# One attention-and-MLP kernel: the opening pair's scores from unsplit float32 keys and queries, with the bias rows as a four-row product

## The chip, the cores and the metric

The kernel runs on one core of one Trainium2 chip. The metric is the time of one execution in device microseconds (us); lower is better. TensorE (PE) multiplies and transposes, VectorE (DVE), ScalarE (ACT) and GpSimd (POOL) work elementwise, SyncE (SP) issues most transfers.

## What is computed

Attention over 4 batches, 8 heads, 576 positions and 64 channels, with a causal mask and a bias from running sums of `s`; then two MLPs of 2304 tokens, 512 channels and 2048 hidden units. Only the attention's scores matter here:

```python
scores = scale * np.matmul(q, k.transpose(0, 1, 3, 2))
s_pos = np.maximum(s, 0.0)
cum = np.cumsum(s_pos, axis=-1)
bias = -(cum[:, :, :, None] - cum[:, :, None, :])
scores = np.where(causal, -1000000000.0, scores + np.minimum(bias, 0.0))
attn = np.exp(scores - np.max(scores, axis=-1, keepdims=True))
```

## The kernel before

The program has three stages on one PE queue: attention (with the first MLP's first part filled in between from the second batch on), the rest of the first MLP, and the second MLP. Attention works on 16 pairs of heads (`g = 4 * b + p`). Each pair has five units, in the order t = 0, 1, 4, 2, 3; a unit is a block of 128 query rows of both heads (t = 4: the last 64 of both heads in one tile), its score tile as wide as the causal mask lets it be: 128, 256, 576 (as two tiles of 288), 384 and 512 columns.

The order on PE is the order in which the code is written (`attention`, a loop over units j). At step j the score tiles of unit j are made (`unit_scores`, L294), three steps later its exponentials are transposed (`unit_transpose`, L341), one step later multiplied with the values (`unit_values`, L391, float32 on both sides). Between them, in the first steps, stand idle products on zeros (`warm`, L80; `idle` in the profile), 128 x 512 each. On the other engines a scheduler orders the instructions within what the code's `behind(...)` fixes.

Scores are made from split numbers. `prep` (L199) transposes a pair's keys and queries on PE (`tk`, `tq`), ACT rounds them to float32r (`hi`, L213: `kh`, `qs`), DVE makes the remainder (`lo`, L216: into the tile `k2` and the lower half of `qs`). So each tile is 96 channel-by-position blocks of 64 x 288: two halves by head, two by position parity. `kh` is doubled into its lower 64 partitions and `qs` into `k2`; for the first two pairs by POOL (`move`, L251), later by a transfer. The tile `k2` carries, below its 64 channel rows, four bias rows: the running sums, split in two, and the constants 1 and -1. `scores_piece` (L279) then makes two float32r products per score tile: `k2` against `k2` (68 rows: cross terms and bias), behind it `kh` against `qs` (128 rows).

```python
for m, (q, k) in enumerate(((k2[:, 1, h], k2[:, 0, h]), (pr["qs"][:, h], pr["kh"][:, h]))):
```

A score tile narrower than 256 columns is made 256 wide (`max(n, 256)`, L315). DVE then adds the mask and takes the row minimum in one instruction (L319), ACT makes the exponential (L326), DVE the reciprocal of the sums (L336), POOL scales (L339).

The opening: `sums` (L104) makes the running sums in two parts, 256 and 320 positions; each part is split by ACT and DVE (`sum_parts`, L125, staged in `stgA`), and four transfers of it per part go from SP into the first pair's bias rows (`open_rows`, L138). The second part's split stands behind the first head's `lo` instructions (`with self.behind(first)`). Behind the opening pair's last POOL copy, POOL itself issues the third pair's loads (`pair_load`, L168, called at L462). All eight PSUM banks have one tag and are taken in turn.

Of the kernel before, what the change touches and what calls it, by code (L numbers as in the profile page):

```python
# [10 lines left out]
F32 = mybir.dt.float32  # L11
F32R = mybir.dt.float32r
# [3 lines left out]
AF = mybir.ActivationFunctionType  # L16
ALU = mybir.AluOpType
# [8 lines left out]
NB, NH, S, D = 4, 8, 576, 64  # L26
NP = NH // 2
NT = NB * S
DM, DF = 512, 2048
P = 128  # L30
# [18 lines left out]
PARTS = ((0, 256), (256, 576))  # L49
ZEROS = 5  # L50
WARM = 6
RUN_ENDS = ((0, 1, 4, 2, 3), (3,), (3,), (3,))
W2_SLOTS = 7
# [8 lines left out]
class Fused:  # L62
# [136 lines left out]
    def prep(self, att, b, p, ld, first=False):  # L199
        nc, ident = self.nc, self.ident  # L200
        h0, h1 = slice(0, D), slice(D, P)

        def new(nm):
            return att.tile([P, 2, S], F32R, name=f"{nm}{b}_{p}", tag=nm, bufs=2)

        g = b * NP + p
        kh, qs, k2 = new("kh"), new("qs"), self.k2[g % 2]
        self.pairs[b, p] = {"kh": kh, "qs": qs, "k2": k2, "ld": ld, "O": None}  # L210

# [18 lines left out]
        def split(*parts):  # L230
# [10 lines left out]
            for i, (high, low, T, scale) in enumerate(jobs):  # L241
                with self.behind((self.parts[1],) if i else ()):
                    lo(low, T, high, scale)

        def main(nm):
            split(*[turn(nm, h) for h in range(2)])

        def move(o, i, hs=(0, 1)):
            if g < 2:
                for h in hs:  # L250
                    self.copied = nc.gpsimd.tensor_copy(o[:, h], i[:, h].bitcast(F32))  # L251
            else:
                nc.sync.dma_start(o.bitcast(F32), i.bitcast(F32))

        if first:
            turned = [[turn(nm, h) for nm in "kq"] for h in range(2)]
            for h in range(2):
                with self.behind(first):
                    split(*turned[h])
                first = tuple(self.parts)  # L260
                if h == 0:
                    with self.behind(first):
                        first = self.sum_parts(PARTS[1])
                move(kh[h1], kh[h0], (h,))
                move(k2[h0, 1], qs[h0], (h,))
            self.warm(WARM)
            return
        if g > 1:
            self.sum_rows(g, self.rows[g])
        main("k")  # L270
        move(kh[h1], kh[h0])
        yield
        main("q")
        move(k2[h0, 1], qs[h0])
        yield
# [3 lines left out]
    def scores_piece(self, u, sc, hs, j0, w):  # L279
        nc = self.nc  # L280
        b, p, t = u
        pr = self.pairs[b, p]
        for h in hs:
            c0, c1 = t * P, (t + 1) * P
            if t == 4:
                c0, c1 = (S - P if h else S - 64), S
            k2 = pr["k2"][: D + 4]
            for m, (q, k) in enumerate(((k2[:, 1, h], k2[:, 0, h]), (pr["qs"][:, h], pr["kh"][:, h]))):
                nc.tensor.matmul(  # L289
                    sc[: c1 - c0, :w], lhsT=q[:, c0:c1], rhs=k[:, j0 : j0 + w],  # L290
                    start=m == 0, stop=m == 1,
                )

    def unit_scores(self, att, u, h):  # L294
        nc = self.nc
# [17 lines left out]
        else:  # L313
            sc = self.bank("S", f"s{b}_{p}_{t}_{h}")
            self.scores_piece(u, sc, (h,), 0, max(n, 256))  # L315
            j0, w = 0, n
# [21 lines left out]
        for i, bt in enumerate(bts):  # L338
            nc.gpsimd.tensor_scalar(bt[:, :n], bt[:, :n], inv[:, i : i + 1], 1.0, ALU.mult, ALU.mult)  # L339

# [92 lines left out]
    def attention(self, att, mlp):  # L433
# [26 lines left out]
        opened = self.moved  # L460
        with self.behind((self.copied,)):
            loads[2] = self.pair_load(att, 0, 2, eng=nc.gpsimd)  # L462
        later.extend(loads[i]["values"] for i in (1, 2))
        for j in range(n + AHEAD + 1):
# [28 lines left out]
            for _ in tr:  # L493
                pass
            if j < n and idx == 4:
                for _ in nprep:
# [513 lines left out]
```

## Time and profile before

| what | value |
| --- | --- |
| median of 3 runs (lowest, highest) | 1022.94 us (1021.01, 1023.03) |
| the profiled execution's own time, its span | 1021.61 us, 1019.6 us |
| PE busy | 998.2 us (98% of the span) |
| DVE, ACT, POOL busy | 797.3, 718.2, 337.8 us |
| chain that ended last, by engine | PE 89%, DVE 4%, DMA 3%, ACT 2%, issue 1% |
| same chain, the scores' products (L289) | 5% |

The span runs from the first to the last instruction; about 2 us of the execution's own time lie outside it. Starts in the trace count from the span's start. Matmuls are pipelined, so a matmul's row is longer than the step to the next one: what a product costs in a row of products is read from the starts. A float32 product stands as two records in the trace, a float32r product and a transpose as one.

### The profile page before, as it was taken

What the parts mean: (1) busy time and instruction counts of PE and PEld (TensorE: products, weight loads), DVE (VectorE), ACT (ScalarE), POOL (GpSimd) and SP (SyncE); (2) the same over time, 40 slices, a digit from 0 to 9 for tenths busy, and PEclk for the clock granted to TensorE, in tenths of its full rate; (3) what the DMA queues carried; (4) which work ended last, traced back from release to release, by engine and by line L of the source; (5) the groups of instructions that cost most, each with busy time, mean ns of one, the idle gap of its engine ahead of it and who ended that gap; (6) DMA issues with size and microseconds to landing.
All of it is one profiled execution on the core that took longest, in us unless ns stands there. A gap on an engine that the chain in (4) does not pass through costs nothing.

```text
span 1019.6 us, 19822 instructions
## 1 busy us (share of the span) xinstructions
PE 998.2 (98%) x7053; PEld 933.9 (92%) x7054; DVE 797.3 (78%) x1804; ACT 718.2 (70%) x1661; POOL 337.8 (33%) x503
## 2 busy tenths in 40 slices
PE   7889999999999999999999999999999999999997
PEld 4679999999999999999999999999999999989996
DVE  7897666766537977777778747998988989889886
ACT  5999889878756655555555436787887777777775
POOL 5778656554410012222111112232222222222222
PEclk9999999999999999999999999999999999999999
DMA  7664564543237546776666644010010100100000
GB/s 180 157 175 100 135 188 146 152 123 72 59 125 247 177 140 196 230 235 224 212 189 235 208 133 190 1 31 32 3 60 1 32 32 1 63 1 1 32 1 32
DMA packets 79074, 115.97 MB, mean 114 GB/s; under 512 B 25552, under 2 KB 63072, under 8 KB 77440
## 3 DMA queue, kind: packets, MB, share of 16 engines
q1 hardware_dynamic: 72640, 94.94, 31.4%
q0 software_dynamic: 6112, 19.47, 5.1%
q8 instruction: 56, 0.92, 0.4%
q14 instruction: 42, 0.34, 0.1%
q10 hardware_dynamic: 224, 0.30, 0.1%
HBM read 74.78 MB, written 31.60 MB: 104 GB/s over the span
## 4 chain that ended last, share of the span: by engine, by line
PE 89%; DVE 4%; DMA 3%; ACT 2%; issue 1%; POOL 0%; SPq 0%; ACTq 0%; DVEq 0%
PE h L638 38%; PE a L815 19%; PE a L662 19%; PE s L289 5%; PE O L406 4%; PE tp L381 3%; DMA raw<-in_moe_w_in_dram 1%; DVE bt L319 1%; DMA x2p<-st 1%; DVE k L216 1%; PE tq L225 1%; PE tk L225 1%; ACT bt L326 0%; PE tp L360 0%; DVE qs L216 0%
## 5 line engine op out<-in xcount | busy, mean ns | idle before, releaser
L638 PE MATMUL h<-x,u 128*128 128x288 f32 x1536 | 231.5, 296 | 1.2 <-ACT st L677 1.2
L662 PE MATMUL a<-gh,u 128*128 128x288 f32 x1024 | 231.7, 297 | 0.0
L638 PEld LDWEIGHTS h<-x,u 128*128 128x128 f32 x1536 | 212.8, 188 | 3.1 <-ACT st L677 1.5
L798 POOL TENSOR_TENSOR gl<-u,gh 128x384 fp32r<-128x384 f32 x96 | 105.7, 1101 | 290.4 <-ACT gh L796 266.4
L662 PEld LDWEIGHTS a<-gh,u 128*128 128x128 f32 x1024 | 173.0, 188 | 1.1 <-issue 0.5
L638 PE MATMUL h<-y,u 128*128 128x384 f32 x864 | 165.7, 336 | 0.0
L638 PEld LDWEIGHTS h<-y,u 128*128 128x128 f32 x864 | 152.9, 188 | 6.2
L662 PE MATMUL a<-gl,u 128*128 128x288 f32 x512 | 150.0, 295 | 0.7 <-DVE gl L655 0.7
L815 PE MATMUL a<-u,gh 128*128 128x512 f32 x432 | 114.6, 394 | 0.9 <-ACT gh L796 0.9
L649 ACT ACTIVATE g<-h 128x288 f32<-128x288 f32 x128 | 52.0, 407 | 75.8 <-PE h L638 75.4
L724 POOL DMA_DIRECT2D x<-xp x64 | 35.3, 552 | 207.3 <-DVE g L650 106.7
L662 PEld LDWEIGHTS a<-gl,u 128*128 128x128 f32 x512 | 96.5, 188 | 1.4 <-DVE gl L655 0.9
L326 ACT ACTIVATE bt<-bt,mn 128x128 f32<-128x128 f32 (+2 forms) x144 | 84.1, 585 | 19.3 <-DVE mn L319 18.2
L815 PEld LDWEIGHTS a<-u,gh 128*128 128x128 f32 x432 | 80.0, 188 | 14.9 <-ACT gh L796 1.8
L339 POOL TENSOR_SCALAR bt<-bt,sm 128x128 f32<-128x128 f32 (+2 forms) x144 | 81.7, 579 | 30.0 <-DVE sm L336 21.6
L796 ACT ACTIVATE gh<-u 128x384 fp32r<-128x384 f32 x96 | 50.6, 527 | 57.6 <-DVE u L794 56.6
L319 DVE CUSTOM_DVE_ANT_0 bt<-s,mask 128x128 f32<-128x128 f32 (+2 forms) x144 | 68.9, 482 | 27.6 <-PE s L289 25.5
L652 ACT ACTIVATE gh<-g 128x288 fp32r<-128x288 f32 x128 | 56.5, 442 | 45.6 <-DVE g L650 43.8
L650 DVE SCALAR_TENSOR_TENSOR g<-g,h 128x288 f32<-128x288 f32 x128 | 57.5, 450 | 29.8 <-ACT g L649 29.2
L781 ACT ACTIVATE y<-h,cf 128x384 f32<-128x384 f32 x96 | 55.4, 577 | 33.9 <-PE h L638 33.9
L786 DVE SCALAR_TENSOR_TENSOR y<-s,cf,y 128x384 f32<-128x384 f32 x96 | 59.3, 618 | 20.6 <-ACT s L783 19.3
L794 DVE SCALAR_TENSOR_TENSOR u<-y,u 128x384 f32<-128x384 f32 x96 | 73.5, 765 | 1.1
(116 smaller groups left out, 2048.0 us busy)
## 6 DMA issues: line engine op xcount, KB each, us to landing
raw<-in_moe_w_in_dram SPq DMA_DIRECT2D x24, 512.0 KB
raw<-in_moe_w_out_dram SPq DMA_DIRECT2D x24, 512.0 KB
x<-xp POOLq DMA_DIRECT2D x64, 144.0 KB, 3.0
wd<-park POOLq DMA_DIRECT2D x36, 256.0 KB, 4.3
u<-wd SPq DMA_DIRECT2D x8, 1024.0 KB
x2p<-st SPq DMA_DIRECT2D x32, 144.0 KB
xp<-x2p SPq DMA_DIRECT2D x32, 144.0 KB
xp<-x SPq DMA_DIRECT2D x32, 144.0 KB
```

Source lines behind the costliest of these rows:

```text
L319: nc.vector.tensor_tensor_reduce(bt[:, j0 : j0 + w], sc[:, :w], mask, 1.0, 3.0e38 if i == 0 else mn[:, 0:1], ALU.add, ALU.min, mn[:, i : i ...
L326: ex = nc.scalar.activation(bt[:, :n], bt[:, :n], AF.Exp, bias=mn[:, i : i + 1], scale=-1.0, accum_out=sm[:, col : col + 1],)
L339: nc.gpsimd.tensor_scalar(bt[:, :n], bt[:, :n], inv[:, i : i + 1], 1.0, ALU.mult, ALU.mult)
L638: nc.tensor.matmul(ps_tile, lhsT=u[:, wl, kk * P : (kk + 1) * P], rhs=x(xl, kk), start=(n == 0), stop=(n == 3 * KD - 1),)
L650: nc.vector.scalar_tensor_tensor(g[:, :w], g[:, :w], 1.0, h, ALU.add, ALU.mult)
L652: self.newest["act"] = nc.scalar.activation(gh[:, :w], g[:, :w], AF.Copy)
L662: nc.tensor.matmul(acc, lhsT=u[:, wl, d * P : (d + 1) * P], rhs=g[gl], start=(first and i == 0), stop=(last and i == 2),)
L781: nc.scalar.activation(y, h, AF.Abs, scale=cf[:, 4:5])
L786: nc.vector.scalar_tensor_tensor(y, s, cf[:, 7:8], y, ALU.mult, ALU.add)
L794: last = nc.vector.scalar_tensor_tensor(p, y, 2.0, p, ALU.subtract, ALU.mult)
L798: nc.gpsimd.tensor_tensor(gl, p, gh.bitcast(F32), ALU.subtract)
L815: nc.tensor.matmul(accs[m], lhsT=g[gl][:, m * P : (m + 1) * P], rhs=u[:, wl, :], start=(f == 0 and i == 0), stop=(f == NF - 1 and i == 2),)
```

## The change

For the opening pair alone (`PLAIN = 1`) the keys and queries are copied from PSUM to float32 tiles (`keep`, lines 248 to 260 of the changed file) and not split; nothing is doubled into lower partitions. Each score tile of that pair is one float32 product over 64 rows, behind it a float32r product over the four bias rows alone, and it is as wide as the mask lets it be (128 columns for t = 0). The second part of the running sums is split behind the second head's key copies. The third pair's loads are issued by POOL behind the first unit's scaling, at step j = 0.

```diff
@@ -49,6 +49,7 @@
 PARTS = ((0, 256), (256, 576))
 ZEROS = 5
 WARM = 6
+PLAIN = 1
 RUN_ENDS = ((0, 1, 4, 2, 3), (3,), (3,), (3,))
 W2_SLOTS = 7
 LEAD = 2
@@ -200,14 +201,16 @@
         nc, ident = self.nc, self.ident
         h0, h1 = slice(0, D), slice(D, P)
 
-        def new(nm):
-            return att.tile([P, 2, S], F32R, name=f"{nm}{b}_{p}", tag=nm, bufs=2)
-
+        g = b * NP + p
+        plain = g < PLAIN
 
+        def new(nm):
+            return att.tile(
+                [P, 2, S], F32 if plain else F32R, name=f"{nm}{b}_{p}", tag=nm, bufs=2
+            )
 
-        g = b * NP + p
         kh, qs, k2 = new("kh"), new("qs"), self.k2[g % 2]
-        self.pairs[b, p] = {"kh": kh, "qs": qs, "k2": k2, "ld": ld, "O": None}
+        self.pairs[b, p] = {"kh": kh, "qs": qs, "k2": k2, "ld": ld, "O": None, "plain": plain}
 
         def hi(out, T, scale):
             self.parts[0] = nc.scalar.activation(out, T, AF.Copy, scale=scale)
@@ -242,36 +245,54 @@
                 with self.behind((self.parts[1],) if i else ()):
                     lo(low, T, high, scale)
 
+        def keep(engs, *parts):
+            done = []
+            for o in range(2):
+                for nm, T, h in parts:
+                    out = (kh if nm == "k" else qs)[h0, h]
+                    out = out.rearrange("p (i t o) -> p o i t", t=3, o=2)[:, o]
+                    src = T[o * D : (o + 1) * D]
+                    scale = 1.0 if nm == "k" else -0.125
+                    if engs[nm] == "act":
+                        done.append(nc.scalar.activation(out, src, AF.Copy, scale=scale))
+                    else:
+                        done.append(nc.vector.tensor_scalar(out, src, scale, None, ALU.mult))
+            return tuple(done)
+
         def main(nm):
-            split(*[turn(nm, h) for h in range(2)])
+            parts = [turn(nm, h) for h in range(2)]
+            if plain:
+                keep({"k": "act", "q": "dve"}, *parts)
+            else:
+                split(*parts)
 
         def move(o, i, hs=(0, 1)):
             if g < 2:
                 for h in hs:
-                    self.copied = nc.gpsimd.tensor_copy(o[:, h], i[:, h].bitcast(F32))
+                    nc.gpsimd.tensor_copy(o[:, h], i[:, h].bitcast(F32))
             else:
                 nc.sync.dma_start(o.bitcast(F32), i.bitcast(F32))
 
         if first:
             turned = [[turn(nm, h) for nm in "kq"] for h in range(2)]
-            for h in range(2):
-                with self.behind(first):
-                    split(*turned[h])
-                first = tuple(self.parts)
-                if h == 0:
-                    with self.behind(first):
-                        first = self.sum_parts(PARTS[1])
-                move(kh[h1], kh[h0], (h,))
-                move(k2[h0, 1], qs[h0], (h,))
+            opened = keep({"k": "act", "q": "act"}, *turned[0])
+            with self.behind((*opened, *first)):
+                keys = keep({"k": "dve"}, turned[1][0])
+                with self.behind(keys):
+                    opened = self.sum_parts(PARTS[1])
+            with self.behind(opened):
+                keep({"q": "act"}, turned[1][1])
             self.warm(WARM)
             return
         if g > 1:
             self.sum_rows(g, self.rows[g])
         main("k")
-        move(kh[h1], kh[h0])
+        if not plain:
+            move(kh[h1], kh[h0])
         yield
         main("q")
-        move(k2[h0, 1], qs[h0])
+        if not plain:
+            move(k2[h0, 1], qs[h0])
         yield
 
 
@@ -284,8 +305,11 @@
             c0, c1 = t * P, (t + 1) * P
             if t == 4:
                 c0, c1 = (S - P if h else S - 64), S
-            k2 = pr["k2"][: D + 4]
-            for m, (q, k) in enumerate(((k2[:, 1, h], k2[:, 0, h]), (pr["qs"][:, h], pr["kh"][:, h]))):
+            k2, qs, kh = pr["k2"][: D + 4], pr["qs"][:, h], pr["kh"][:, h]
+            terms = ((k2[:, 1, h], k2[:, 0, h]), (qs, kh))
+            if pr["plain"]:
+                terms = ((qs[:D], kh[:D]), (k2[D:, 1, h], k2[D:, 0, h]))
+            for m, (q, k) in enumerate(terms):
                 nc.tensor.matmul(
                     sc[: c1 - c0, :w], lhsT=q[:, c0:c1], rhs=k[:, j0 : j0 + w],
                     start=m == 0, stop=m == 1,
@@ -312,7 +336,7 @@
             i = h
         else:
             sc = self.bank("S", f"s{b}_{p}_{t}_{h}")
-            self.scores_piece(u, sc, (h,), 0, max(n, 256))
+            self.scores_piece(u, sc, (h,), 0, n if self.pairs[b, p]["plain"] else max(n, 256))
             j0, w = 0, n
             mask = self.mask[:, 640 - n : 640]
             i = 0
@@ -336,7 +360,9 @@
         rc = nc.vector.reciprocal(inv[:, c], inv[:, c])
         self.tail = (ex, rc)
         for i, bt in enumerate(bts):
-            nc.gpsimd.tensor_scalar(bt[:, :n], bt[:, :n], inv[:, i : i + 1], 1.0, ALU.mult, ALU.mult)
+            self.normed = nc.gpsimd.tensor_scalar(
+                bt[:, :n], bt[:, :n], inv[:, i : i + 1], 1.0, ALU.mult, ALU.mult
+            )
 
     def unit_transpose(self, att, u):
         nc, ident = self.nc, self.ident
@@ -458,9 +484,7 @@
             with self.behind((self.moved,)):
                 self.store_sums()
         opened = self.moved
-        with self.behind((self.copied,)):
-            loads[2] = self.pair_load(att, 0, 2, eng=nc.gpsimd)
-        later.extend(loads[i]["values"] for i in (1, 2))
+        later.append(loads[1]["values"])
         for j in range(n + AHEAD + 1):
             i, k = j - AHEAD, j - AHEAD - 1
             self.zeros = j < ZEROS
@@ -492,6 +516,10 @@
             self.fill(q / 3, j < 4)
             for _ in tr:
                 pass
+            if j == 0:
+                with self.behind((self.normed,)):
+                    loads[2] = self.pair_load(att, 0, 2, eng=nc.gpsimd)
+                later.append(loads[2]["values"])
             if j < n and idx == 4:
                 for _ in nprep:
                     pass
```

The scheduled order of three places, by the built programs. First DVE from the second scan of the running sums (`cum`) to the first score tile's minimum (`bt_0_0_0`, `mn`); names end in serial numbers, `k_0` is the first `k2` tile, `ISA` the minimum. Before (each L216 row stands there twice, for the two parities):

```order
L118 SCALAR_TENSOR_TENSOR cum<-s_114,cum,nz 32x320
L216 SCALAR_TENSOR_TENSOR k_0_134<-tk_0_0_152,kh_0_150 64x288
L216 SCALAR_TENSOR_TENSOR qs_0_151<-tq_0_0_156,qs_0_151 64x288
L130 TENSOR_TENSOR stgA<-cum,stgA 32x320
L216 SCALAR_TENSOR_TENSOR k_0_134<-tk_0_1_160,kh_0_150 64x288
L216 SCALAR_TENSOR_TENSOR qs_0_151<-tq_0_1_164,qs_0_151 64x288
L319 ISA bt_0_0_0_216,mn_0_0_0_217<-s_0_0_0_218,mask 128x128
```

The same stretch of DVE in the changed kernel:

```order
L118 TENSOR_SCALAR s_114<-s_114 32x320
L119 SCALAR_TENSOR_TENSOR cum<-s_114,cum,nz 32x320
L259 TENSOR_SCALAR kh_0_150<-tk_0_1_160 64x288 x2
L131 TENSOR_TENSOR stgA<-cum,stgA 32x320
L343 ISA bt_0_0_0_200,mn_0_0_0_201<-s_0_0_0_202,mask 128x128
```

Eight remainders have gone and two copies have come; ahead of the second part's split (L130, now L131) stand two instructions in place of four, and nothing stands between it and the first minimum.

Second, POOL from the masks to the first scaling (`bt_0_0`; `kn_2` and `qn_2` are the third pair's keys and queries). Before (the two L251 rows stand there twice):

```order
L162 AFFINE_SELECT mask<-mask 64x64
L251 CAST kh_0_150<-kh_0_150 64x576
L251 CAST k_0_134<-qs_0_151 64x576
L181 DMA kn_2_211<-in_k_dram 96x2x384
L181 DMA qn_2_213<-in_q_dram 96x2x384
L339 TENSOR_SCALAR bt_0_0_0_216<-bt_0_0_0_216,sm_0_0_215 128x128
L339 TENSOR_SCALAR bt_0_0_1_227<-bt_0_0_1_227,sm_0_0_215 128x128
```

The same stretch of POOL in the changed kernel, to the second pair's first copy:

```order
L163 AFFINE_SELECT mask<-mask 64x64
L363 TENSOR_SCALAR bt_0_0_0_200<-bt_0_0_0_200,sm_0_0_199 128x128
L363 TENSOR_SCALAR bt_0_0_1_211<-bt_0_0_1_211,sm_0_0_199 128x128
L182 DMA kn_2_223<-in_k_dram 96x2x384
L182 DMA qn_2_225<-in_q_dram 96x2x384
L272 CAST kh_1_236<-kh_1_236 64x576 x2
```

The four copies have gone, and the two loads stand behind the first unit's scaling.

Third, DVE where the second pair begins: from the last unit's sums of the opening pair (`sm_0_3`) to the minimum of the second pair's unit t = 1 (`bt_1_1_0`); L561 to L563 convert a weight, L361 and L365 copy transposes of t = 4. Before:

```order
L336 RECIPROCAL sm_0_3_353<-sm_0_3_353 128x2
L561 TENSOR_SCALAR stgA<-stgA 128x512
L361 COPY pt_119<-tp_0_4_0_423 128x512
L562 TENSOR_SCALAR stgA<-stgA 128x512
L319 ISA bt_1_0_1_429,mn_1_0_1_430<-s_1_0_1_431,mask 128x128
L365 COPY pt_119<-tp_0_4_1_440 64x128
L216 SCALAR_TENSOR_TENSOR k_0_134<-tk_2_0_406,kh_2_402 64x288
L563 SCALAR_TENSOR_TENSOR stgA<-stgA 128x512
L319 ISA bt_1_1_0_448,mn_1_1_0_449<-s_1_1_0_450,mask 128x256
L216 SCALAR_TENSOR_TENSOR k_0_134<-tk_2_1_410,kh_2_402 64x288
```

The same stretch of DVE in the changed kernel (each L219 row stands there twice):

```order
L360 RECIPROCAL sm_0_3_341<-sm_0_3_341 128x2
L589 TENSOR_SCALAR stgA<-stgA 128x512
L590 TENSOR_SCALAR stgA<-stgA 128x512
L387 COPY pt_119<-tp_0_4_0_411 128x512
L343 ISA bt_1_0_1_417,mn_1_0_1_418<-s_1_0_1_419,mask 128x128
L591 SCALAR_TENSOR_TENSOR stgA<-stgA 128x512
L391 COPY pt_119<-tp_0_4_1_428 64x128
L219 SCALAR_TENSOR_TENSOR k_0_134<-tk_2_0_394,kh_2_390 64x288
L219 SCALAR_TENSOR_TENSOR k_0_134<-tk_2_1_398,kh_2_390 64x288
L343 ISA bt_1_1_0_436,mn_1_1_0_437<-s_1_1_0_438,mask 128x256
```

The copy of t = 4 stands behind two weight instructions in place of one, and the minimum of `bt_1_1_0` behind all four remainders of the third pair's keys in place of one. Work is the same; PE's order differs from before in the opening pair's products alone.

## Rows read from the trace of the kernel before

**Rows 1.** Windows: stretch, length, busy us of PE, PEld, DVE, ACT, POOL, PEclk, DMA.
```profile
9.30:16.10 6.80, 4.23 (x24) 2.60 (x24) 4.89 (x17) 3.41 (x13) 3.93 (x7) 1.00 0.58 154
16.10:23.00 6.90, 6.90 (x46) 5.01 (x47) 6.20 (x23) 4.05 (x13) 2.99 (x6) 1.00 0.76 187
23.00:30.00 7.00, 4.25 (x39) 3.13 (x39) 5.24 (x21) 6.90 (x20) 5.08 (x7) 1.00 0.90 206
30.00:38.00 8.00, 8.00 (x86) 6.45 (x83) 7.89 (x29) 7.46 (x22) 4.71 (x9) 1.00 0.76 186
...
100.00:150.00 50.00, 50.00 (x468) 48.65 (x466) 34.19 (x114) 43.18 (x124) 30.45 (x50) 1.00 0.57 155
```

**Rows 2.** Timeline of PE, 9 to 19 us: start, length, then [idle before <-releaser].
```profile
9.29 0.36 PE L289 MATMUL s<-k 68*128 68x256 f32 x1 [1.02 <-DMA k<-stgA]
...
9.61 1.04 PE L82 MATMUL idle<-mask 128*128 128x512 bf16 x4
11.62 0.35 PE L289 MATMUL s<-k 68*128 68x256 f32 x1 [0.97 <-POOL k L251]
...
13.06 0.66 PE L225 MATMUL tk<-ident,spare 96*128 96x96 f32 x6
...
16.03 0.37 PE L289 MATMUL s<-k 68*128 68x288 f32 x1 [1.41 <-DMA k<-stgA]
```

**Rows 3.** Groups by line, 5.2 to 12.04 us: count, busy us, mean ns.
```profile
L216 DVE SCALAR_TENSOR_TENSOR qs<-tq,qs 64x288 fp32r<-64x288 f32 x4 | 1.8, 457 | 0.1
L216 DVE SCALAR_TENSOR_TENSOR k<-tk,kh 64x288 fp32r<-64x288 f32 x4 | 1.8, 454 | 0.2
L213 ACT ACTIVATE kh<-tk 64x288 fp32r<-64x288 f32 x4 | 1.7, 427 | 0.4 <-PE tk L225 0.3
```

**Rows 4.** Timeline of DVE, 9 to 16.5 us.
```profile
9.16 0.95 DVE L130 TENSOR_TENSOR stgA<-cum,stgA 32x320 fp32r<-32x320 f32 x1
...
12.05 0.29 DVE L319 CUSTOM_DVE_ANT_0 bt<-s,mask 128x128 f32<-128x128 f32 x1
```

**Rows 5.** Timeline of SP's transfer issues, 5.9 to 12.6 us (two answers).
```profile
6.00 2.66 SPq L136 DMA_DIRECT2D k<-stgA  x4
...
10.13 2.36 SPq L136 DMA_DIRECT2D k<-stgA  x4
```

**Rows 6.** The chain that ended last, in order of time, 0 to 60 us.
```profile
11.94 3.96 DMA k<-stgA
```

**Rows 7.** Timeline of PE, 20 to 60 us: products and transposes in a row.
```profile
24.77 0.66 PE L406 MATMUL O<-pt,vn 128*64 128x128 f32 x8
...
29.77 0.80 PE L406 MATMUL O<-pt,vn 128*64 128x64 f32 x20
...
34.59 1.09 PE L406 MATMUL O<-pt,vn 128*64 128x128 f32 x16
...
35.95 0.40 PE L289 MATMUL s<-kh,qs 128*128 128x512 f32 x1
36.19 0.60 PE L381 MATMUL tp<-ident,bt 128*128 128x128 f32 x4
```

**Rows 8.** The same timeline of PE, where the second pair begins.
```profile
22.07 0.38 PE L289 MATMUL s<-k 68*128 68x256 f32 x1
...
23.83 0.66 PE L360 MATMUL tp<-ident,bt 128*128 128x128 f32 x4 [0.76 <-POOL bt L339]
...
29.32 0.52 PE L381 MATMUL tp<-ident,bt 128*128 128x128 f32 x3 [0.74 <-DVE mn L319]
```

**Rows 9.** Timeline of DVE, 20 to 45 us.
```profile
23.18 0.67 DVE L319 CUSTOM_DVE_ANT_0 bt<-s,mask 128x512 f32<-128x512 f32 x1
...
26.11 0.43 DVE L561 TENSOR_SCALAR stgA<-stgA 128x512 f32<-128x512 f32 x1 [0.76 <-ACT stgA L560]
```

**Rows 10.** Timeline of ACT, 20 to 45 us: the last exponential of the opening pair.
```profile
24.14 0.72 ACT L326 ACTIVATE bt<-bt,mn 128x512 f32<-128x512 f32 x1
```

**Rows 11.** DMA issues, 0 to 45 us: count, KB each, us from issue to landing.
```profile
qn<-in_q_dram POOLq DMA_DIRECT2D x1, 288.0 KB, 4.3
```

## The prediction

> **What bounds the kernel now.** I read the table of windows first. From the second batch on the kernel is a stream of products: PE is busy for the whole of 100 to 150 us [rows 1], so a piece that the start saves or costs is carried to the end unless a later wait takes it up. The first 38 us are another matter. Between 9.3 and 16.1 us PE is busy for 4.23 of 6.80 us, from 16.1 to 23.0 all the time, from 23 to 30 only 4.25 of 7.00, and there ACT is full (6.90); from 30 to 38 DVE is nearly full (7.89 of 8.00) [rows 1]. So the start is a relay: first a wait, then PE, then ACT, then DVE. The clock column says 1.00 in all these windows, TensorE's upper level of 2.4 GHz, so prices need no correction for it.
>
> The timeline of PE names the waits of the first stretch: 1.02 us for bias rows ahead of the first score tile at 9.29, 0.97 us ahead of the second tile at 11.62, and 1.41 us for the second part's bias rows ahead of unit t = 4 at 16.03 [rows 2]. The chain of waits says the same of the last: 3.96 us from the fourth of that part's issues, at 11.94, to its landing [rows 6]. Those four issues begin at 10.13 [rows 5] because DVE makes the low half of the sums only at 9.16 to 10.11 [rows 4], behind four remainders of 0.45 us [rows 3].
>
> **What it removes at the front.** DVE loses eight remainders of 0.45 us, 3.6 us, and gets two copies; ACT makes six copies in place of eight roundings; POOL loses four copies. A copy on DVE is not in the trace; ACT's of the same 64 x 288 block takes 0.43, DVE's two-input remainder 0.45 [rows 3]; I take 0.4 for it, and either end moves nothing, since what follows waits for SP. The low half of the second part then stands behind two copies, not four remainders: about 0.9 us sooner, start by 8.3. It took 0.95 us [rows 4], so it is done by 8.7 to 9.2. SP's first four issues end at 8.66 [rows 5], so the second four begin at about 8.7 in place of 10.13, and their last is issued at 11.94 - 1.43 = 10.5. Landing takes 2.4 us at best (second issue of the first four at about 6.9, product at 9.29 [rows 2, 5]) and 3.96 at worst [rows 6]: 12.9 to 14.5. I take 12.9, because the third pair's two 288 KB loads, which POOL issued just ahead in the kernel before, now leave after the first unit's scaling, at some 13 us.
>
> The first minimum, at 12.05 before [rows 4], waited for DVE's queue of remainders, not for its tile of 9.3 to 9.8. It can now run at about 9.6, and ACT's first exponential with it.
>
> **What it adds on PE.** Price of a float32r column: the 512-column product at 35.95 is followed at 36.19 [rows 7], 0.24 us, 0.47 ns a column. Price of a float32 column: sixteen records of the value products took 1.09 us, eight 0.66 [rows 7]; the two heads' halves run side by side, so eight records are four steps, 0.43 / 4 = 0.108 us for 128 columns, 0.84 ns a column and record. Twenty records of 64 columns took 0.80: nine steps of 0.054 and the same 0.33 of start and drain give 0.81, so the step goes with the columns. A float32 product is two records: 1.68 ns a column. The transposes, float32 and full width, go by the same 0.11 us for 128 columns [rows 7], so I use it for the 128-wide products too. The other ends: if the halves did not overlap, a record costs half of it, 0.84 ns a column and product; above, I allow the 0.16 us that the first step of such a row can lose, at each of twelve tiles no more than 1 us in all.
>
> Before, a tile's two products cost 0.94 ns a column; now 1.68 + 0.47 = 2.15, so 1.21 ns more. Unit t = 0 is half as wide as before, 0.28 us against 0.24. A float32r product of 128 columns is not in the trace: 0.06 us by columns, 0.22 if it were priced as float32; twice 0.16 at most.
>
> **PE's walk.** First tile's bias product at 9.29 as before, since the rows it waits for are issued at the same times. Then, with 0.22 us for each idle product (four take 1.04 with a drain of 0.38 [rows 2]): four of them, to 10.2; second tile 0.28, to 10.5 (its rows, issued by 8.1, are there 2.4 later); two idle, 10.9; t = 1 first head, 256 x 2.15 = 0.55, 11.5; six transposes 0.5 [rows 2], 12.0; idle and second head, 12.75; two idle, 13.2. So t = 4 starts at 13.2 if its rows are there, 2.8 us before 16.03 [rows 2], and at 14.5 at worst.
>
> From there to the second pair's first product it took 22.07 - 16.03 = 6.04 us [rows 2, 8] without a wait [rows 1]. Units 4, 2 and 3 hold 1152 + 768 + 1024 = 2944 columns, so 3.57 us more: 9.61. The second pair's product starts at 22.8, 0.7 **later** than before. PE pays back more than the opening gave it.
>
> **Why I still forecast a small gain.** PE's lead was not used there. At 23.83 PE stood 0.76 us for POOL, at 29.32 for 0.74 us for a minimum [rows 8]: 2.75 us idle in that window [rows 1]. What set it was DVE and ACT, late from the opening: the last score tile was done about 0.3 us ahead of 22.07, but DVE took its minimum at 23.18 [rows 9], and ACT its exponential at 24.14 [rows 10], with ACT then full. With the change that tile is done at 22.5, DVE has run ahead and takes it at once (0.67 [rows 9], and 0.1 to read out), and ACT starts at about 23.4: 0.7 us sooner. ACT's weight conversion behind it releases DVE's at 26.11 [rows 9], and DVE is full from there to 38: the 0.7 goes on. The new order of DVE costs some of PE's slack in two places (one more weight instruction ahead of the copy of t = 4, three more remainders ahead of the minimum that 29.32 waited for, some 0.3 to 0.5 us each), none of DVE's total; the 2.75 us idle cover it, and without that cover it would cost up to 0.5.
>
> POOL's loads, moved from under the opening to about 13.3, land 4.3 us after their issue [rows 11], under 19; PE turns them after 22.8. SP's later transfers all go out 1.4 us sooner and cost nothing by that.
>
> Sum: **-0.7 us** against the profiled execution's 1021.61, so 1020.9; that execution stands 1.3 below the median of the runs, and against the median of 1022.94 it is **1022.2**. A measurement of this kernel can tell about 0.2%, 2.05 us, from no change: faster is below 1020.9, slower above 1025.0.
>
> **Rivals.**
> - *The bias product hides* (faster). Its four rows lie in other partitions than the 64 of the float32 product. The trace shows two heads' products running side by side in two halves of the columns: sixteen records in eight steps [rows 7]; it shows none in two groups of rows. If it happens, 0.47 ns a column is off the path, 1.4 us over 2944 columns and 0.2 in t = 1: -2.3, 1020.6. A float32 price at its lower end would reach as far, since then DVE and ACT limit. The Trainium skill, TensorE: Matmul & The Clock Gate, Part 3 on packing small matmuls, says that products whose operands sit in different row groups overlap almost wholly; by that rule the time would be that of this rival. Against it: both products add to the same tile. Chance 0.20.
> - *The rows land as late as before* (slower). If the second part's transfers meet other traffic (the values' and the next pairs' loads, which the DMA column shows 58% busy in that window [rows 1]) and land at 15.9, t = 4 starts at 16.03 and the 3.57 us stand alone: each microsecond after 13.2 costs one, the gain is gone at 13.9, and at 16.0 it is +2.1, 1025.0. For it: their wait was 3.96 where the first part's was 2.4. Against it: they leave 1.4 us sooner and ahead of POOL's loads. Chance 0.10.
> - *It is taken up later*: the 0.7 ends in a later wait for a transfer or in the new order of DVE: 0, 1022.9. PE's full windows speak against it, ACT's and DVE's full and reordered queues for it. Chance 0.15.
> - The forecast, 1022.2: 0.55. Its own spread, by landing at 12.9 to 14.5, runs from -0.7 to +0.6.
>
> **How the numbers follow.** Faster: the first rival's 0.20 and 0.06 of the forecast, whose runs spread by 1 us to either side: 0.26. Slower: most of the second rival: 0.07. Same: 0.67. The range reaches from the first rival less 1 us of run spread, 1019.6, to the late landing, 1023.5, with 0.8 of the same: 1024.3.
>
> **What would show it.** First minimum at about 9.6 and not 12.05; SP's second four issues from 8.7; t = 4 at 13.2 on PE with no wait for rows; float32 products of 256 columns at 0.43 us; the second pair's first product near 22.8, later than before, yet ACT's last exponential of the opening near 23.4. Wrong: a wait for rows ahead of t = 4; a bias product that starts within some 10 ns of a float32 one and adds no time; a second pair that starts before 22.

## The result, and the profile after

The change makes the kernel 1.0% slower: 1032.39 us median (1030.40 to 1034.77, six executions) against 1022.45 (1020.96 to 1023.03, six), a ratio of 1.0102 with a 95% interval of 1.0082 to 1.0121. The prediction of 1022.2 us was wrong, in sign and by 10 us, and its range missed it. The profiled execution took 1034.4 us, span 1032.6.

First the windows, with the columns of [rows 1]; the last row has other bounds.

```profile
9.30:16.10 6.80, 6.64 (x30) 3.23 (x29) 1.78 (x11) 2.93 (x12) 1.54 (x3) 1.00 0.33 90
16.10:23.00 6.90, 6.90 (x22) 2.85 (x23) 4.76 (x14) 2.89 (x9) 4.13 (x8) 0.76 0.95 211
23.00:30.00 7.00, 7.00 (x13) 2.13 (x11) 1.95 (x8) 1.42 (x5) 0.74 (x1) 0.50 0.79 165
30.00:38.00 8.00, 8.00 (x24) 4.11 (x24) 2.02 (x9) 2.91 (x7) 1.36 (x3) 0.50 0.02 4
...
19.70:40.20 20.50, 20.50 (x55) 8.97 (x54) 7.88 (x27) 7.46 (x20) 4.81 (x8) 0.50 0.51 114
```

PE, which stood 2.57 of the first 6.80 us and 2.75 of 23 to 30 before [rows 1], is busy for 6.64 of the first and full in the next three. From 23 to 30 us, where ACT was full before, DVE and ACT are busy for 1.95 and 1.42 of 7.00 us: the relay has become PE alone. And the clock column, 1.00 everywhere before, reads 0.50 from 19.7 to 40.2 us, the level of 1.2 GHz. The timeline of PE over the same stretch, to set beside [rows 2, 8]:

```profile
12.76 0.70 PE L313 MATMUL s<-kh,qs 64*128 64x256 f32 x2
13.38 0.38 PE L313 MATMUL s<-k 4*128 4x256 f32 x1
...
16.03 0.75 PE L313 MATMUL s<-kh,qs 64*128 64x288 f32 x2
...
28.65 2.07 PE L313 MATMUL s<-kh,qs 64*128 64x512 f32 x2
30.66 0.79 PE L313 MATMUL s<-k 4*128 4x512 f32 x1
...
36.11 0.58 PE L313 MATMUL s<-k 68*128 68x256 f32 x1
```

A 256-column float32 product starts at 12.76 and its bias product 0.62 us later; t = 4 starts at 16.03 as before, though no longer behind a wait; a float32 product of 512 columns, at the low clock, holds PE from 28.65 to 30.66; the second pair's first product stands at 36.11, 14.0 us later than the 22.07 of [rows 8]. The loss is whole by the time when PE turns to the first MLP. Its first product, in the timelines of the kernel before and after:

```profile
78.52 0.96 PE L638 MATMUL h<-x,u 128*128 128x288 f32 x6
```
```profile
92.22 0.96 PE L666 MATMUL h<-x,u 128*128 128x288 f32 x6
```

13.7 us later there, 13.0 in the span: whatever is lost ahead of that place is kept, as the prediction said of PE's full windows.

### The profile page after: what moved, and what is told of

Its sections match the earlier page's. It is cut to its first block, busy times and chain, and to the rows that moved or that the text cites. A ratio compares the mean times of both kernels' runs of the same rounds, so it can differ in the third digit from the quotient of the medians.

```text
span 1032.6 us, 19834 instructions
## 1 busy us (share of the span) xinstructions
PE 1016.8 (98%) x7065; PEld 939.5 (91%) x7066; DVE 796.4 (77%) x1798; ACT 718.5 (70%) x1659; POOL 334.0 (32%) x499
## 4 chain that ended last, share of the span: by engine, by line
PE 91%; DVE 4%; ACT 1%; DMA 1%; POOL 1%; issue 1%; ACTq 0%; DVEq 0%; POOLq 0%
PE h L666 38%; PE a L843 19%; PE a L690 18%; PE s L313 6%; PE O L432 4%; PE tp L407 3%; PE idle L83 1%; DVE bt L343 1%; PE tk L228 1%; DVE k L219 1%; PE tq L228 1%; PE tp L386 1%; DMA x2p<-st 1%; DVE stgA L591 0%; DMA raw<-in_moe_w_out_dram 0%
```

## Experiments

Each kernel is compared with the kernel before as run beside it on the same chip; that had medians of 1022.41, 1022.68, 1022.88 and 1022.14 us in the four groups of runs.

### Which part of a step is dear: rows, type, or the change of rows

Three theories: products on few rows are dear and let the clock fall; float32 products do; or each **change of rows** from one product to the next exposes work that is otherwise hidden. Four kernels vary rows and type. First float32r instead of float32:

```diff
-                [P, 2, S], F32 if plain else F32R, name=f"{nm}{b}_{p}", tag=nm, bufs=2
+                [P, 2, S], F32R, name=f"{nm}{b}_{p}", tag=nm, bufs=2
```

> The opening pair's keys and queries are copied to float32r tiles instead of float32 ones, so that a score tile is one float32r product on 64 rows and the float32r product on the four bias rows. It leaves out the remainders that float32 would keep. Few rows (products on 64 and 4 of the 128 rows let the granted clock fall): the clock falls to 0.50 again somewhere between 15 and 40 us, time 1027 to 1031. Float32 (it is the two-record float32 products that let it fall): clock 1.00 all the way, time 1022 to 1025. On the step: if each change of the number of rows makes the weight load wait for the product ahead (0.2 us each, twice a tile), a 256-column tile takes 0.11 + 0.11 + 0.09 for each product, 0.6 us, against 0.93 in the changed kernel and 0.25 before; if only float32 was dear, 0.25.

Measured: 1029.97 us (1028.87 to 1032.19), ratio 1.0075 [1.0056, 1.0093]. Timeline of PE and a window:

```profile
14.13 0.38 PE L313 MATMUL s<-kh,qs 64*128 64x256 f32 x1
14.44 0.38 PE L313 MATMUL s<-k 4*128 4x256 f32 x1
14.75 0.61 PE L83 MATMUL idle<-mask 128*128 128x512 bf16 x2
```
```profile
16.10:23.00 6.90, 6.90 (x20) 3.19 (x19) 4.78 (x15) 2.65 (x8) 3.96 (x7) 0.53 1.03 251
```

0.31 us for either product, 0.62 for the tile, the same on 64 rows as on four; and the clock fell from 16.5 us on without any float32. Float32 is not what was overlooked.

Second, all rows:

```diff
+                for x in (kh, qs):
+                    nc.gpsimd.memset(x[h1], 0.0)
...
-                terms = ((qs[:D], kh[:D]), (k2[D:, 1, h], k2[D:, 0, h]))
+                terms = terms[::-1]
```

> The changed kernel with all its products on as many rows as the array has: the lower halves of the float32 tiles and the channel rows of the bias tile are set to zero, so that the float32 product runs over 128 rows and the bias product over 68. Few rows: the clock stays 1.00, and the time comes down to 1021 to 1024. Float32: the clock falls to 0.50 as in the changed kernel, 1028 or more. On the step: if the change of rows is what exposes the loads, a 256-column tile takes 0.43 + 0.11 + 0.03 = 0.57 us; if a float32 product is that dear anyway, still about 0.9.

Measured: 1029.44 us (1026.14 to 1030.77), ratio 1.0061 [1.0041, 1.0080]. Timeline of PE and a window:

```profile
13.33 0.59 PE L318 MATMUL s<-kh,qs 128*128 128x256 f32 x2
13.57 0.47 PE L318 MATMUL s<-k 68*128 68x256 f32 x1
13.89 0.61 PE L83 MATMUL idle<-mask 128*128 128x512 bf16 x2
...
24.39 0.39 PE L318 MATMUL s<-k 68*128 68x256 f32 x1
```
```profile
30.00:38.00 8.00, 7.21 (x53) 6.16 (x52) 6.06 (x21) 6.22 (x16) 4.28 (x7) 0.57 0.75 173
```

The step is 0.56 us, as the prediction had priced it, and the second pair starts at 24.39, with the clock at 1.00 to 30.9; the changed kernel, in an execution at full clock (below), started it at 27.77. So the change of rows was the dear part. The time did not follow: the clock fell behind 30 us instead, and the 1021 to 1024 expected were missed.

Third, one product:

```diff
-                terms = ((qs[:D], kh[:D]), (k2[D:, 1, h], k2[D:, 0, h]))
+                terms = ((pr["qs"][: D + 4, h], pr["kh"][: D + 4, h]),)
...
+            x = d[2 - 2 * i : 4 - 2 * i, i] if g else self.opening[i][D + 2 - 2 * i : D + 4 - 2 * i]
```

> The bias rows are put under the float32 keys and queries, so that a score tile is one float32 product on 68 rows and no bias product. Few rows: 68 rows with half of the products gone; the clock stays 1.00 if 68 rows count as the full array, as the k2 product of the kernel before did, and the time is 1020 to 1023; otherwise it falls. Float32: the clock falls, 1026 or more. On the step: 256 columns in 0.43 to 0.46 us if the change of rows is what exposes the loads, 0.62 if float32 exposes them.

Measured: 1023.21 us (1020.67 to 1029.50, ten executions), ratio 1.0009 [0.9992, 1.0026]. Timeline of PE:

```profile
13.34 0.60 PE L321 MATMUL s<-kh,qs 68*128 68x256 f32 x2
13.77 0.60 PE L83 MATMUL idle<-mask 128*128 128x512 bf16 x2
...
22.84 0.39 PE L321 MATMUL s<-k 68*128 68x256 f32 x1
```

0.43 us for 256 columns, 1.68 ns a column, and the second pair at 22.84: the price of a float32 column in the prediction was right. 68 rows count as the full array here.

Fourth, 64 rows throughout, the rows not changing between score and idle products:

```diff
+        r = D if self.pairs else P
...
-                self.idle_bank, lhsT=self.idle[:, :P], rhs=self.idle, start=True, stop=True
+                self.idle_bank, lhsT=self.idle[:r, :P], rhs=self.idle[:r], start=True, stop=True
```

> One float32 product per score tile as in the kernel with 68 rows, but on 64 rows, and the idle products behind the first transposes on 64 rows too. It leaves out the opening pair's bias rows. Products on 64 rows now follow each other without a change of rows; only the transposes and the value products still stand between them. Few rows (the clock counts rows in use): the clock falls to 0.50 before 23 us, as in the changed kernel, time 1026 to 1031. Exposed loads (it is the time in which PE waits for weights that lets the clock fall): those are mostly gone, the clock stays 1.00 to 30 us or more, as with 68 rows, time 1021 to 1024. On the step: 0.43 us for 256 columns where an idle product of 64 rows stands ahead, 0.62 behind transposes.

Measured: 1020.88 us (1019.51 to 1036.70, eight executions), ratio 0.9996 [0.9959, 1.0033], without the highest. Two executions, 1033.67 and 1036.70, had mean clocks of 1.000 and 0.998; what made them long is not known. Timeline of PE and a window:

```profile
11.19 0.59 PE L322 MATMUL s<-kh,qs 64*128 64x256 f32 x2
11.62 0.59 PE L84 MATMUL idle<-mask 64*128 64x512 bf16 x2
...
21.45 0.39 PE L322 MATMUL s<-k 68*128 68x256 f32 x1
```
```profile
16.10:23.00 6.90, 6.90 (x37) 3.68 (x35) 4.79 (x20) 4.54 (x12) 3.00 (x6) 1.00 0.96 241
```

Again 0.43 us, and the clock held to 85.8 us in this profile. **Few rows** falls as a theory of the step, and as one of the clock so far as this profile and the mean clocks of all eight executions (0.997 to 1.000) tell; the change of rows stands.

Where the time of a change goes is seen in the timeline of the weight loads, of the kernel before and of the changed kernel in an execution at full clock (told below):

```profile
35.72 0.19 PEld L289 LDWEIGHTS s<-kh,qs 128*128 128x128 f32 x1
35.96 0.59 PEld L381 LDWEIGHTS tp<-ident,bt 128*128 128x128 f32 x4
```
```profile
11.73 0.29 PEld L313 LDWEIGHTS s<-kh,qs 64*128 64x128 f32 x2 [0.42 <-issue]
12.36 0.18 PEld L313 LDWEIGHTS s<-k 4*128 4x128 f32 x1 [0.33 <-issue]
```

Before, the load at 35.72 runs 0.23 us ahead of its product at 35.95 [rows 7], beside the product ahead. In the changed kernel the load of the bias product begins at 12.36, when the product itself begins, and PEld stood idle for 0.33 us ahead of it. What that is worth is read from three kernels: 256 float32 columns take 0.43 us where the rows don't change and 0.63 here (11.73 to 12.36); 256 float32r columns are 0.12 us by the step of [rows 7], and 0.31 in both kernels with few rows. So **each change of rows costs 0.20 us** with 128 weight columns, and the two that fall in a tile's own step 0.40. The Trainium skill, TensorEngine Tiling (Array Packing), Key Properties, says that changing the tiling mode drains the engine; the trace agrees, and shows that a load stands in the open as well.

### Is it the product on four rows?

The clock fell early in the two kernels that had a four-row product. Two kernels part this from the 64-row one: the bias on 68 rows with zero channels behind a float32 product on 64 (`terms[0]` is the product of `k2` against `k2`), and float32 on all rows ahead of the bias on four.

```diff
-                terms = ((qs[:D], kh[:D]), (k2[D:, 1, h], k2[D:, 0, h]))
+                terms = ((qs[:D], kh[:D]), terms[0])
```

> The changed kernel with the float32 product on 64 rows as it is, and the bias product on 68 rows, the channel rows of its tile set to zero: no product on four rows is left, but the rows still change between float32 product, bias product and idle product. Exposed loads: a 256-column tile takes two loads, one or two drains and its columns, 0.85 to 0.93 us, and the clock falls to 0.50 before 30 us, 1027 to 1034. If the product on four rows is what lets the clock fall: the clock stays 1.00 to 30 us or more as in the kernel with all rows, 1023 to 1027.

Measured: 1032.38 us (1029.45 to 1033.23), ratio 1.0087 [1.0070, 1.0103]; second pair at 28.26, clock 1.00 to 34.3 us. Timeline of PE:

```profile
12.89 0.70 PE L316 MATMUL s<-kh,qs 64*128 64x256 f32 x2
13.52 0.39 PE L316 MATMUL s<-k 68*128 68x256 f32 x1
13.75 0.66 PE L228 MATMUL tk<-ident,spare 96*128 96x96 f32 x6
```

0.86 us, and the time of the changed kernel, without a four-row product. Each expectation is half right: the step and the time are those of the exposed loads, but the clock held for longer than that theory said.

```diff
-                terms = ((qs[:D], kh[:D]), (k2[D:, 1, h], k2[D:, 0, h]))
+                terms = ((qs, kh), (k2[D:, 1, h], k2[D:, 0, h]))
```

> The float32 product on all 128 rows (lower halves zero), the bias product on its four rows alone: as many changes of rows as in the kernel with the float32 product on 64 rows and the bias product on 68, but here the product on few rows is the four-row one. Exposed loads alone: a 256-column tile 0.43 + 0.09 + 0.11 + 0.11 + 0.09 = 0.83 us, the second pair's first product at 27.5 to 29 and the clock held as in that kernel, to 30 us or more. Four-row product: the same step, but the clock falls to 0.50 before 23 us and the second pair starts behind 30.

Measured: 1029.70 us (1028.59 to 1032.80), ratio 1.0081 [1.0059, 1.0103]. Timeline of PE:

```profile
11.40 0.59 PE L318 MATMUL s<-kh,qs 128*128 128x256 f32 x2
11.93 0.38 PE L318 MATMUL s<-k 4*128 4x256 f32 x1
12.24 0.71 PE L228 MATMUL tk<-ident,spare 96*128 96x96 f32 x6
...
26.00 0.39 PE L318 MATMUL s<-k 68*128 68x256 f32 x1
```

0.84 us against 0.83 expected; the float32 product, whose rows don't differ from those ahead, takes 0.53, so 0.10 of a change's 0.20 is the wait for the product ahead to be out, in that product's step, and the rest the load. The second pair at 26.00 is earlier than expected, since here a float32 product behind a full-row one pays no change; the clock held to 48.3 us, so the four-row product doesn't by itself let it fall.

### The change of rows in the kernel before

```diff
+        r = D if self.pairs else P
...
-                self.idle_bank, lhsT=self.idle[:, :P], rhs=self.idle, start=True, stop=True
+                self.idle_bank, lhsT=self.idle[:r, :P], rhs=self.idle[:r], start=True, stop=True
```

> The kernel before, and nothing of the change: only the idle products behind the first transposes run on 64 rows instead of 128, so that rows change at both ends of each group of them. Exposed loads: each group of idle products costs PE two loads and two drains, 0.4 us, some 1.6 to 2 us between 16 and 22 us; PE waits less ahead of 16 us, so part of it is hidden there; the clock falls in more of the executions or for longer than before; 1023.5 to 1027. If the change of rows costs nothing by itself, 1021 to 1023.5 as before.

Measured: 1030.49 us (1030.34 to 1031.71), ratio 1.0076 [1.0063, 1.0089]. Windows:

```profile
9.30:16.10 6.80, 6.04 (x21) 3.23 (x21) 3.76 (x13) 2.38 (x9) 3.22 (x6) 0.61 0.56 161
16.10:23.00 6.90, 6.90 (x23) 3.65 (x21) 4.79 (x16) 2.95 (x9) 3.46 (x6) 0.50 0.81 202
23.00:30.00 7.00, 7.00 (x21) 3.19 (x20) 3.08 (x12) 3.45 (x9) 1.89 (x3) 0.50 0.40 107
```

3.5 us above the upper end of what was expected, from nothing but the rows of products whose result nobody reads. The clock was low from 10.9 to 34.8 us in this profile, and three of the four executions had a mean clock of 0.987 or 0.988; but the fourth, the longest, had 1.000 at 1031.71 us. How much is the clock and how much the loads, these runs don't part.

### Chance of the execution

The changed kernel, the kernel with 64 and 68 rows and the kernel before were each profiled once more, without an edit.

> The changed kernel once more, for the clock's place in a second execution. If the opening's products let it fall, it falls to 0.50 between 14 and 24 us again; if the first profile was a chance one, it holds to 30 us and the second pair's first product stands at 28 to 29 instead of 36.

Measured: 1026.65 us, clock 1.00 from 4.9 us on. Timeline of PE and windows:

```profile
6.34 1.46 PE L83 MATMUL idle<-mask 128*128 128x512 bf16 x6
...
9.34 0.29 PE L313 MATMUL s<-k 4*128 4x128 f32 x1 [1.12 <-DMA k<-stgA]
...
11.20 0.61 PE L83 MATMUL idle<-mask 128*128 128x512 bf16 x2
11.73 0.70 PE L313 MATMUL s<-kh,qs 64*128 64x256 f32 x2
12.36 0.38 PE L313 MATMUL s<-k 4*128 4x256 f32 x1
12.67 0.72 PE L228 MATMUL tk<-ident,spare 96*128 96x96 f32 x6
...
15.00 0.75 PE L313 MATMUL s<-kh,qs 64*128 64x288 f32 x2
...
27.77 0.39 PE L313 MATMUL s<-k 68*128 68x256 f32 x1
```
```profile
16.10:23.00 6.90, 6.90 (x27) 2.94 (x27) 4.93 (x17) 3.03 (x8) 3.23 (x7) 1.00 0.99 251
23.00:30.00 7.00, 7.00 (x41) 3.73 (x40) 2.85 (x12) 3.70 (x9) 2.12 (x4) 1.00 0.61 129
```

This execution parts the two losses. At full clock the change costs 1026.65 - 1021.61 = 5.0 us, one execution against one (the kernel before spread from 1020.65 to 1022.71 where its mean clock was 0.999 or more), and the second pair starts 5.7 later than before. The first profile's 1034.4 is 7.8 above it, its second pair 8.3: that is the clock. The other executions go with it: 1030.4 us at a mean clock of 0.996, 1030.9 at 0.993 to 0.994, 1033.9 to 1034.8 at 0.989 to 0.990.

One part of the clock's loss the clock column doesn't show. Its records begin at 4.9 us here, at 9.5 in the first profile, and it reads 1.00 ahead of them too, though PE runs at half speed there. The same six idle products in the first profile:

```profile
7.59 2.39 PE L83 MATMUL idle<-mask 128*128 128x512 bf16 x6
```

They take 2.39 us in place of 1.46, and t = 4 starts at 16.03 in place of 15.00: of the 8.3 us, 1.0 stands there. A mean clock of 1.000 therefore doesn't exclude a start at half speed.

> The kernel with the float32 product on 64 rows and the bias product on 68 once more. If it is the four-row product that lets the clock fall in the opening, the clock holds to 28 us again; if the first profile was a chance one, it falls before 24 us.

Measured: 1031.07 us; the clock held to 33.6 us again and then fell, the second pair at 28.01.

> The kernel before once more. Its executions had mean clocks from 0.994 to 1.000, its profile 1.00 from 6.5 us on. Where the mean clock is 0.996 or less, one or two stretches at 0.50 stand between 10 and 75 us, next to PE's waits, and the time is 1022.5 to 1024.5; where it is 0.999 or more, none, and 1021 to 1022.

Measured: 1022.62 us at a mean clock of 0.996. Windows:

```profile
9.30:16.10 6.80, 5.60 (x22) 3.94 (x23) 4.20 (x14) 2.57 (x10) 3.65 (x6) 0.66 0.54 146
16.10:23.00 6.90, 6.90 (x37) 5.01 (x35) 5.82 (x20) 3.75 (x11) 3.45 (x6) 0.84 0.72 179
```

The clock was low from 11.5 to 18.3 us, and the second pair starts at 23.40, 1.3 later than in the profile that the prediction was read from. The kernel before had lost some clock in most of its executions (mean 0.994 to 1.000); its profile was one of the few without.

### The other parts of the change

The sums' second part ahead of all remainders, in the kernel before:

```diff
+            with self.behind(first):
+                first = self.sum_parts(PARTS[1])
             for h in range(2):
                 with self.behind(first):
                     split(*turned[h])
                 first = tuple(self.parts)
-                if h == 0:
-                    with self.behind(first):
-                        first = self.sum_parts(PARTS[1])
```

> The kernel before, with one part of the change alone: the second part of the running sums is split ahead of all remainders. The split products stay. If the order of the sums is worth what the prediction gave it, SP's second four issues begin at about 8.7 in place of 10.13 and the unit t = 4 starts at about 14.6 in place of 16.03; with ACT and DVE as limits behind it the time is 1021 to 1022.5. If the order cost anything, 1023 or more. The clock stays 1.00 by every theory.

Measured: 1024.22 us (1023.33 to 1025.27), ratio 1.0017 [1.0007, 1.0026]. PE waited 2.27 us for POOL's copy ahead of the first tile, now at 10.16 in place of 9.29, and the clock was low from 11.9 to 18.7 and from 29.0 to 35.8. The same with more idle products in those waits (`WARM` 14, `fill` 8 in place of 4):

> The kernel before with the second part of the sums split ahead of the remainders, and with 14 idle products in place of 6 ahead of the first score tile and 8 in place of 4 ahead of the second, where PE waited. If the early sums alone were slower only because PE's longer wait let the clock fall, the clock is 1.00 behind 10 us, t = 4 starts at about 14.6 and the time is 1020.5 to 1022. If the order of the sums costs time by itself, 1023 or more at a clock of 1.00.

Measured: 1027.06 us (1025.27 to 1029.51), ratio 1.0048 [1.0033, 1.0062], with the clock at 1.00 from 4.8 to 28.7 us and at 0.50 behind that to 35.5. t = 4 started at 14.81, 1.2 earlier, yet the second pair at 22.64, 0.6 later (timeline of PE):

```profile
10.19 0.35 PE L288 MATMUL s<-k 68*128 68x256 f32 x1 [0.58 <-POOL k L251]
...
20.98 0.89 PE L380 MATMUL tp<-ident,bt 128*128 128x128 f32 x4 [1.27 <-POOL bt L338]
```

The remainders stand behind the sum now and POOL's copies behind them, and PE waits for POOL at both places. The expected 1021 to 1022.5 and 1020.5 to 1022 were missed: early sums alone are no gain here. That they would be one with the remainders gone as well is not shown.

The loads alone (POOL issues the third pair's behind the first scaling):

```diff
-        with self.behind((self.copied,)):
-            loads[2] = self.pair_load(att, 0, 2, eng=nc.gpsimd)
...
+            if j == 0:
+                with self.behind((self.normed,)):
+                    loads[2] = self.pair_load(att, 0, 2, eng=nc.gpsimd)
```

> The kernel before, with one part of the change alone: POOL issues the third pair's loads behind the first unit's scaling. If the loads have no part in the result, 1021 to 1023.5, the same as before, with the third pair's transposes not waiting for them. If their place costs time, PE waits for them behind 22 us and the time is 1024 or more.

Measured: 1021.73 us (1021.35 to 1022.99), ratio 0.9994 [0.9985, 1.0003]: no part in it.

### A version without the loss

The kernel with one product on 68 rows, taken to two pairs and to four (`PLAIN = 2`, `PLAIN = 4`; the bias rows of each pair under its own keys and queries):

> The first two pairs by one float32 product on 68 rows. Each such pair takes about 2 us more on PE, and eight remainders off DVE less four copies (1.9 us), and four POOL copies of the doubled halves. DVE and ACT were the limits from 23 to 60 us: if they still are, 1019 to 1021.5; if PE is the limit there, 1023 to 1025.

Measured: 1021.48 us (1020.85 to 1023.51), ratio 0.9991 [0.9981, 1.0001]; and again, in more executions:

> The kernel with the first two pairs on 68 rows once more, for a narrower interval: 1020.9 to 1021.9, a ratio of 0.9985 to 0.9995 to the kernel before, and a clock that falls in fewer executions than before, since PE waits less between 23 and 30 us.

Measured: 1021.51 us (1020.53 to 1023.20, twelve executions), ratio 0.9988 [0.9979, 0.9996]; mean clocks 0.998 to 1.000. A window:

```profile
23.00:30.00 7.00, 6.29 (x62) 4.58 (x61) 6.23 (x22) 6.93 (x22) 3.73 (x6) 1.00 1.06 218
```

PE works for 6.29 of the 7.00 us in which it stood 2.75 before [rows 1], and ACT is full as it was. 0.1% is little: this interval lies just below 1, those of the first measurement and of the four pairs below reach it.

> All four pairs of the first batch by one float32 product on 68 rows. If DVE and ACT are still the limit from 38 to 75 us, 1019 to 1021; if PE is by then the limit (it was busy for 26.7 of 29 us there with two such pairs, and each pair adds about 2 us), 1022 to 1024.

Measured: 1021.83 us (1021.27 to 1024.17), ratio 0.9992 [0.9983, 1.0002]: the third and fourth pair bring nothing more.

## Why the prediction was wrong, step by step

- **The front came as predicted, at full clock.** In that execution SP's second four issues begin at 8.76 (8.7 predicted), the first minimum runs at 9.78 (9.6), the first bias product follows a wait for its rows at 9.34 (9.29), and t = 4 has no wait for rows. The late-rows rival did not come about.
- **The price of a column was right**: 1.68 ns for float32 (0.43 us for 256 columns on 68 rows, where it stands alone). The 0.43 us of 512 float32r columns behind it, from 24.75 in the full-clock execution, are the 0.24 priced and 0.19 of a change.
- **The step that failed is the bound that stood beside it**: "the 0.16 us that the first step of such a row can lose, at each of twelve tiles no more than 1 us in all". That loss was taken from the value products, where the shape changes in columns, and named as an upper end that entered neither the sum nor the range (and twelve times 0.16 is 1.9, not 1). Two changes of rows fall in a tile's own step, each 0.20: 0.40 a tile, 4.8 for twelve. Eight tiles, some 3.2, stand behind the start of t = 4 (12.77 us to the second pair in place of 9.61, 3.16 more). Ahead of it stand three and the first one's bias product, 1.4; the rest of the 1.8 us there (15.00 in place of 13.2) is the change from full rows to 64, of which 0.09 shows in the step of each of four idle products: the two from 11.20 take 0.53 to 11.73, by 0.22 each 0.44. 22.8 + 1.8 + 3.16 gives the 27.8 measured.
- **So the gain had no place to show.** DVE and ACT were free early, and stood waiting for PE's tiles: ACT's last exponential of the opening, forecast for 23.4, begins at 28.31 in that execution, and at 36.39 in the first profile. The forecast's -0.7 became +5.0.
- **The second step that failed**: "The clock column says 1.00 in all these windows [...] so prices need no correction for it". One execution had shown that of the kernel before; the column says nothing of a changed kernel, and not even of other executions of the same one. The clock made the other half of the loss: median 1032.39 less 1026.65 is 5.7 us. (The two halves make 10.7 and not 9.9, since the median of the kernel before has 0.8 of low clock in it too.)
- **The hiding rival** is refuted: the bias product starts 0.63 us behind the float32 one, when that is out, and adds 0.31. The Trainium skill, TensorE: Matmul & The Clock Gate, Part 3, lets products in different row groups overlap; these lie in different rows and do not. That they are of different shapes (64 rows and four), or add to one tile, are two possible reasons, and no run here parts them. Nor was anything taken up later: the first MLP starts 13.7 us late, and the span is 13.0 longer.
- **What stays open** is what lets the clock fall in one execution and not in the next. It is neither float32 nor few rows nor the four-row product by itself (the profiles of the kernels with one product on 68 rows, with one on 64 rows, and with all rows ahead of four held it through the opening), and not PE's idle time as the profile counts it: from 9.30 to 11.51 us PE was busy for 1.35 in the execution of the kernel before that held it, for 1.36 in the one that lost it at 11.51, and float32r on 64 rows lost it with PE full. All five kernels whose rows change in the opening had a median of 1029.7 us or more, but the one on 128 rows came to 1029.4 as well, and its clock fell only behind 30 us. So the cost of a change on PE is shown, at the step and at the second pair; that the changes also bring the clock down is not.

## What to carry to other kernels

Price a product by its neighbour as well as by its columns: where its rows (4, 64, or all, among which 68 and 96 counted here) differ from those of the product ahead, PE waits for that product to be out and its weight load isn't hidden, 0.2 us a change at full clock. Keep small extra terms inside the same product (four bias rows under 64 channels cost nothing; as a product of their own they made a tile of 256 columns 0.94 us instead of 0.43). Before "the clock is 1.00" enters a sum, look at the clock of several executions, and at where its records begin, and give a fall of it a chance of its own.

## What was not expected of the hardware

The same program took 1026.65 and 1034.4 us, and the granted clock is what differs: 1.00 from 4.9 us on in one; in the other half speed to 9.5 us and 0.50 from 19.7 to 40.2, with PE busy for all of 16 to 30 us in both. Changing the rows of idle products, whose results are never read, cost the kernel before 0.76%. And a product on four rows takes as long as one on 64: 0.31 us each for 256 columns.
